# Fewer idle matmuls, and the load of v, its copies and two softmax steps moved, in an attention + feed-forward kernel on Trainium2

## Chip, cores, metric

The kernel runs on one core of one Trainium2 chip. The metric is the device time of one execution in microseconds (us).

In the profile's lines PE is the tensor engine (matmuls), PEld its weight loads, DVE VectorE, ACT ScalarE, POOL GpSimd and SP SyncE; L424 is line 424 of the kernel. `...` marks lines left out.

## The reference

Cross-covariance attention over the channels, then a feed-forward layer with a tanh GELU. There are 4 batches of 6080 rows and 256 channels; the hidden width is 2048.

```python
qn = q / (norm(q, axis=1) + 1e-6);  kn = k / (norm(k, axis=1) + 1e-6)
s = kn.transpose(0, 2, 1) @ qn / tau          # 256 x 256 for each batch
a = exp(s - s.max(-1));  a /= a.sum(-1) + 1e-9
x = (v @ a).reshape(24320, 256)
out = gelu_tanh(x @ w_in) @ w_out
```

The kernel folds `a @ w_in` into one matrix aW for each batch, so that a block of 512 rows of v needs one product with aW (first product) and one with W_out (second product, done with seven smaller products).

## The kernel before

Only the parts that the argument touches. At the start the Gram matrix of batch 0 is built from seven chunks of q and k, as they land. `warm(n)` issues n matmuls on zeros, whose results nobody reads, to keep the tensor engine busy.

```python
WARM = [0, 6, 10, 12, 14, 14, 0]
for c in range(nch):                    # nch = 7 chunks of batch 0
    ...                                 # loads, casts
    if 1 <= c < nch - 1:
        ss_rows(c - 1, 0); ss_rows(c - 1, 1)   # column sums of the squares, on the tensor engine
        warm(WARM[c])
    squares(0, c); fold_rows(0, c)
    if c == nch - 2:
        ss_rows(c, 0)
    if c == nch - 1:
        ss_rows(c, 0); q_factor(); ss_rows(c - 1, 1)
    for i in range(len(rows_of(0, c))):
        gram_row(0, c, i)
    if c == nch - 1:
        ss_rows(c, 1)
...                                     # loads of W_in, v, W_out: see the diff
pe_vt(0, "r")       # v of block 0: 8 transposes on the tensor engine, 2 copies on VectorE
warm(14)
scores(0)           # ACT: lnk, rk; VectorE: S = G * rk; ACT: eT = exp(S * rq)
first_aw()          # row sums of eT, aW of batch 0
```

Then 48 blocks of 512 rows (448 in the last of each batch) run, each in eight steps p. Step p of block n does a part of the first product of block n and of the second product of block n - 1. In between, the next batch is prepared: its chunks are loaded, squared and multiplied in blocks 0 to 8 of the batch, its norms taken in block 9 (`k_row` leaves the diagonal matrix dg), its exponentials in block 10 (`scores_c` does a reciprocal of a quarter in each of four steps, and eT in the last), and aW in block 11.

```python
if blk == 9:
    if p == 3: ss_cols(nxt); norms(nxt)
    if p == 7: k_row(nxt)
if blk == 10:
    if p == 0: k_row_pe(nxt)            # tensor engine: broadcast of dg (L350)
    if p == 1: scores_b(nxt)            # ACT: tanh
    if p in (2, 4, 6, 7): scores_c(nxt, (2, 4, 6, 7).index(p))
if blk == 11:
    if p == 0: row_sums(nxt)            # tensor engine: sums of eT (L386)
    aw_part(nxt, p // 2, p % 2, ...)
```

A record per line follows: L213 Gram rows, L231 and L237 sums of squares, L322 idle matmuls, L285 and L288/L289 transposes of v and their copies, L261 and L263 the logarithm and the factor rk of the k norms on ScalarE, L267 scores, L302 row sums of batch 0, L400 aW, L424 first product, L520 second product, L536 and L544 its additions and transpositions on VectorE.

Of the kernel before, what the change touches and what calls it, by code (L numbers as in the profile page):

```python
# [17 lines left out]
def kernel(  # L18
# [102 lines left out]
    def load_qk(b, c):  # L121
        load_one(b, c, 0)
        load_one(b, c, 1)
# [134 lines left out]
    def scores(b):  # L258

        lnk = smx.tile([128, 256], FP32, tag="lnk")  # L260
        nc.scalar.activation(lnk, SS[1], AF.Ln, bias=eps)  # L261
        rk = smx.tile([128, 256], FP32, tag="rk")
        nc.scalar.activation(rk, lnk, AF.Exp, scale=-0.5)  # L263
        S = smx.tile([128, 2, 256], FP32, tag="S")
        eT = smx.tile([128, 2, 256], BF16, tag="eT")
        for jc in range(2):
            nc.vector.tensor_mul(S[:, jc, :], G[b][:, jc, :], rk)  # L267
        for jc in range(2):
            nc.scalar.activation(eT[:, jc, :], S[:, jc, :], AF.Exp, scale=RQ[0][:, jc : jc + 1])
        ET[b] = eT  # L270
# [3 lines left out]
    def load_v0(n):  # L274
        t = yout.tile([128, BLK // 128, C], BF16, tag="ot", name=f"v{n}")
        V0.append(t)
        nc.gpsimd.dma_start(out=t, in_=v[0, n * BLK : n * BLK + BLK, :].rearrange(
            "(s p) c -> p s c", p=128))

    def pe_vt(n, tag):  # L280

        ps = pM.tile([128, 2, BLK], BF16, tag=tag, name=f"vt_ps{n}")
        for s in range(BLK // 128):
            for cc in range(2):
                nc.tensor.transpose(ps[:, cc, s * 128 : s * 128 + 128],  # L285
                                    V0[n][:, s, cc * 128 : cc * 128 + 128], ident_bf)
        vT = vts.tile([128, 2, BLK], BF16, tag="vT", name=f"vT_pe{n}")
        nc.vector.tensor_copy(vT[:, 0, :], ps[:, 0, :])  # L288
        nc.vector.tensor_copy(vT[:, 1, :], ps[:, 1, :])  # L289
        vt_tiles[n] = vT  # L290
# [27 lines left out]
    def warm(n):  # L318

        w = pH.tile([128, 2, 512], FP32, tag="h", name="warm")  # L320
        for i in range(n):
            nc.tensor.matmul(w[:, 0, 0:256], lhsT=ones_bf, rhs=zeros_bf, start=True, stop=True)  # L322
# [42 lines left out]
    def scores_c(b, step):  # L365

        th = TH[b]
        if step == 0:
            dn = smx.tile([128, 2, 256], FP32, tag="S")
            DN[b] = dn  # L370
            nc.vector.tensor_scalar(dn, th, -1.0, 1.0, op0=ALU.mult, op1=ALU.add)
        dn = DN[b]
        piece = dn[:, step // 2, step % 2 * 128 : step % 2 * 128 + 128]
        nc.vector.reciprocal(piece, piece)  # L374
        if step == 3:
            eT = smx.tile([128, 2, 256], BF16, tag="eT")
            nc.vector.scalar_tensor_tensor(eT, th, 1.0, dn, op0=ALU.add, op1=ALU.mult)
            ET[b] = eT
# [247 lines left out]
    with tc.manual_schedule():  # L626
        first = load_first()
        load_qk(0, 1)
        load_qk(0, 2)
        ident = const.tile([128, 128], FP32)  # L630
        make_identity(nc, ident)
        ones_bf = const.tile([128, 128], BF16)
        nc.vector.memset(ones_bf, 1.0)
        zeros_bf = const.tile([128, 256], BF16)
        nc.vector.memset(zeros_bf, 0.0)
        ones_f = const.tile([128, 128], FP32)
        nc.vector.memset(ones_f, 1.0)
        eps = const.tile([128, 1], FP32)
        nc.vector.memset(eps, 1e-12)
        halves = const.tile([128, 4], FP32)  # L640
        nc.vector.memset(halves, 0.5)
        log_it = const.tile([128, 1], FP32)
        nc.vector.memset(log_it, math.log(inv_tau))
        ident_bf = const.tile([128, 128], BF16)
        nc.vector.tensor_copy(ident_bf, ident)
        nc.scalar.preload_act_table_set("natural_log_exp_and_others")

        win_bf = const.tile([128, 2, D], BF16)
        wcomb = const.tile([128, 7, 8, 128], BF16)
        nch = len(chunks_of(0))  # L650
        WARM = [0, 6, 10, 12, 14, 14, 0]
        for c in range(nch):
            if c == 0:
                cast_first(first)
            if c >= 3:
                load_qk(0, c)
            if 1 <= c < nch - 1:
                ss_rows(c - 1, 0)
                ss_rows(c - 1, 1)
                warm(WARM[c])  # L660
            squares(0, c)
            fold_rows(0, c)
# [4 lines that stand above are left out]
                q_factor()  # L667
                ss_rows(c - 1, 1)
            for i in range(len(rows_of(0, c))):
                gram_row(0, c, i)  # L670
            if c == nch - 1:
                ss_rows(c, 1)
        wi = moe_w_in.rearrange("(c p) d -> p c d", p=128)
        for fs in range(4):
            nc.gpsimd.dma_start(out=win_bf[:, :, fs * 512 : fs * 512 + 512],
                                in_=wi[:, :, fs * 512 : fs * 512 + 512])
            if fs == 0:
                load_v0(0)
        load_v0(1)
        load_wout()  # L680
        load_v0(2)
        pe_vt(0, "r")
        warm(14)
        scores(0)
        first_aw()
        nc.scalar.preload_act_table(AF.Gelu_apprx_tanh)
        aw_part(0, 1, 0, "dve", "a")
        aw_part(0, 1, 1, "dve", "r")

        NN = B * NB  # L690
        for n in range(NN):
            b, blk = divmod(n, NB)
            nxt = b + 1
            for p in range(PAIRS):
                if n >= 1:
                    keeps(n - 1, p)
                if p == 0 and PE_BLOCKS <= n + 2 < NN:
                    load_vt(n + 2)
                gate = mm1(n, p)
                if n == 1 and p in (0, 3):  # L700
                    prep_wout(2 + p // 3)
                if p == 0 and n + 3 < NN:
                    cast_v(n + 3, gate)
                if n == 0 and p in (1, 3):
                    fs = 2 + p // 2
                    aw_part(0, fs, 0, "dve", "q")
                    aw_part(0, fs, 1, "dve", "p")
                if n == 0 and p in (6, 7):
                    prep_wout(p - 6)
                if n >= 1:  # L710
                    mm2(n - 1, p)
                    if p == 1:
                        sums_2(n - 1, 4, 8)
                        if n == 1:
                            prep_wout(4)
                    if p == PAIRS - 1:
                        store(n - 1)
                if p == 5:
                    sums_1(n)
                    if n + 1 < PE_BLOCKS:  # L720
                        pe_vt(n + 1, "q")
                if p == 7:
                    sums_2(n, 0, 4)
                if nxt < B:
                    ncn = len(chunks_of(nxt))
                    if p in (2, 5) and blk < ncn:
                        load_one(nxt, blk, p // 5, gate)
                    c = blk - 1
                    if 0 <= c < ncn:
                        if p == (4 if n == 1 else 0):  # L730
                            squares(nxt, c)
                        if p >= 2:
                            gram_row(nxt, c, p - 2)
                        if p == (6 if n == 1 else 3):
                            sum_rows(nxt, c)
                    if blk == 9:
                        if p == 3:
                            ss_cols(nxt)
                            norms(nxt)
                        if p == 7:  # L740
                            k_row(nxt)
                    if blk == 10:
                        if p == 0:
                            k_row_pe(nxt)
                        if p == 1:
                            scores_b(nxt)
                        if p in (2, 4, 6, 7):
                            scores_c(nxt, (2, 4, 6, 7).index(p))
                    if blk == 11:
                        if p == 0:  # L750
                            row_sums(nxt)
                        aw_part(nxt, p // 2, p % 2, "act" if p in (1, 4, 5, 6) else "dve")
        mm2_last(NN - 1)
# [35 lines left out]
```

## Time and profile before

| | before |
|---|---|
| median of 4 runs | 726.29 us (726.0 to 726.41) |
| span of the profiled run | 724.6 us |
| tensor engine busy | 693.5 us, 96% |
| granted clock | 1.000 |

The prediction below shows the main lines: the engines, the chain that ended last, the tensor engine's waits and the start's timeline. Three more places come from the timeline of the kernel before; the columns are start us, us, engine, line, operation, tiles, shapes, count, and in brackets the idle time ahead and what ended it.

```profile
41.40 1.89 PE L424 MATMUL hp<-vT_pe,aw 128*128 128x512 bf16 x8
...
61.95 1.03 PE L520 MATMUL r<-t,wcomb 128*128 128x256 bf16 x8 [0.70 <-DVE c L536]
...
183.92 0.70 PE L350 MATMUL ps<-dg,ones_f 128*128 128x256 f32 x2 [0.60 <-DVE dg L344]
```

The first block's products begin at 41.40. At 61.95 the tensor engine still waits for VectorE, which has been busy without a gap since 48.9. After that, all its waits of note are the two kinds at each batch change, of which 183.92 is one.

### The profile page before, as it was taken

The page shows a single profiled execution, that of the slowest core. Times are in us where ns is not written, and L with a number is a line of the kernel's source. Part 1 is how long each engine was busy: PE and PEld are TensorE (multiplying, and loading weights), DVE is VectorE, ACT ScalarE, POOL GpSimd, SP SyncE. Part 2 cuts the span into 40 slices and gives each one's busy share as a digit, 9 for nine tenths or more (in the row PEclk, how much of TensorE's full clock was granted, in tenths as well). Part 3 has the DMA queues.
Part 4 walks back from the last instruction along what each step waited for, and adds up shares of the span by engine and source line. Part 5 has one row for each costly group of instructions (what it writes and reads, how often), then busy time and mean ns, then how long its engine had stood idle before and what let it go on. Part 6 is the DMA issues. An engine that isn't in the chain of part 4 may idle for free.

```text
span 724.6 us, 12205 instructions
## 1 busy us (share of the span) xinstructions
PE 693.5 (96%) x4808; PEld 472.0 (65%) x4896; DVE 508.8 (70%) x904; ACT 486.0 (67%) x593; POOL 70.2 (10%) x131
## 2 busy tenths in 40 slices
PE   3899999999899999999999999999999999999997
PEld 2756666666566666666666666666665666666665
DVE  4479878785866787878676878778587465564565
ACT  4377667766667677667667776677666767666673
POOL 4221011100001111010000111011000000000000
PEclk9999999999999999999999999999999999999999
DMA  9995968963548788786436887889344546546233
GB/s 241 201 245 91 157 108 137 140 100 57 91 71 135 115 140 133 122 120 100 72 59 93 137 140 116 131 125 126 57 71 75 86 58 97 79 78 96 43 59 56
DMA packets 161706, 78.93 MB, mean 109 GB/s; under 512 B 149408, under 2 KB 152736, under 8 KB 160672
## 3 DMA queue, kind: packets, MB, share of 16 engines
q0 software_dynamic: 13936, 39.46, 34.6%
q1 hardware_dynamic: 147088, 37.52, 31.4%
q10 hardware_dynamic: 624, 1.16, 0.5%
q8 instruction: 38, 0.62, 0.3%
q14 instruction: 20, 0.16, 0.1%
HBM read 78.91 MB, written 36.57 MB: 159 GB/s over the span
## 4 chain that ended last, share of the span: by engine, by line
PE 87%; DVE 6%; DMA 4%; issue 1%; POOL 1%; ACT 0%; DVEq 0%; POOLq 0%
PE hp L424 41%; PE r L520 22%; PE p L520 11%; PE q L520 6%; PE G L213 4%; DMA t<-in_k_dram 2%; DMA v<-in_v_dram 2%; PE ps L400 2%; DVE ot L544 1%; DVE dn L374 1%; DVE t L504 1%; DVE t L502 1%; DVE t L503 1%; DVE c L536 0%; POOL t L93 0%
## 5 line engine op out<-in xcount | busy, mean ns | idle before, releaser
L428 ACT ACTIVATE g<-hp 128x1024 bf16<-128x1024 f32 (+1 forms) x384 | 387.4, 1015 | 200.6 <-PE hp L424 186.8
L424 PE MATMUL hp<-vT,aw 128*128 128x512 bf16 (+1 forms) x1363 | 353.9, 377 | 2.7
L520 PEld LDWEIGHTS <-wcomb 128*128 128x128 bf16 x2688 | 262.6, 98 | 98.8 <-issue 1.8
L424 PEld LDWEIGHTS <-aw 128*128 128x128 bf16 x1536 | 150.0, 98 | 109.3 <-issue 1.1
L520 PE MATMUL r<-t,wcomb 128*128 128x256 bf16 (+1 forms) x1152 | 148.1, 271 | 1.2 <-DVE c L536 0.7
L536 DVE TENSOR_TENSOR c<-r,y 128x256 f32<-128x256 f32 (+1 forms) x95 | 40.1, 422 | 58.3 <-PE r L520 51.0
L536 DVE TENSOR_TENSOR c<-q,x 128x256 f32<-128x256 f32 (+1 forms) x48 | 20.0, 417 | 71.6 <-PE q L520 69.8
L213 PE MATMUL G<-t 128*128 128x256 bf16 (+1 forms) x368 | 64.8, 273 | 1.1 <-DMA t<-in_k_dram 1.1
L504 DVE TENSOR_TENSOR t<-t,g 128x1024 bf16<-128x1024 bf16 (+1 forms) x96 | 65.2, 679 | 0.0
L503 DVE TENSOR_TENSOR t<-g 128x1024 bf16<-128x1024 bf16 (+1 forms) x96 | 65.0, 677 | 0.0
L502 DVE TENSOR_TENSOR t<-g,t 128x1024 bf16<-128x1024 bf16 (+1 forms) x96 | 63.5, 661 | 0.0
L544 DVE STREAM_TRANSPOSE ot<-c 128x256 f32<-128x256 f32 (+1 forms) x144 | 57.6, 425 | 1.7
L491 DVE TENSOR_TENSOR t<-g 128x2048 bf16<-128x2048 bf16 (+1 forms) x48 | 57.8, 1204 | 0.0
L132 POOL DMA_DIRECT2D vb<-in_v_dram x45 | 22.6, 502 | 359.0 <-PE hp L424 359.0
L520 PE MATMUL r<-g,wcomb 128*128 128x256 bf16 (+1 forms) x384 | 49.3, 271 | 1.4
L165 ACT ACTIVATE sq<-t 128x1536 bf16<-128x1536 bf16 (+3 forms) x29 | 43.7, 1506 | 9.8 <-DMA t<-in_q_dram 9.8
L520 PE MATMUL p<-g,wcomb 128*128 128x256 bf16 (+1 forms) x384 | 49.3, 271 | 0.0
L520 PE MATMUL q<-g,wcomb 128*128 128x256 bf16 (+1 forms) x384 | 49.3, 271 | 0.0
L520 PE MATMUL p<-t,wcomb 128*128 128x256 bf16 (+1 forms) x384 | 49.3, 271 | 0.0
L544 DVE STREAM_TRANSPOSE ot<-r 128x256 f32<-128x256 f32 (+1 forms) x48 | 21.3, 443 | 33.1 <-PE r L520 33.1
L213 PEld LDWEIGHTS <-t 128*128 128x128 bf16 (+1 forms) x368 | 35.5, 98 | 11.2 <-issue 2.7
L529 ACT ACTIVATE y<-p 128x256 f32<-128x256 f32 (+1 forms) x95 | 36.3, 382 | 0.7 <-ACT x L529 0.4
(101 smaller groups left out, 341.2 us busy)
## 6 DMA issues: line engine op xcount, KB each, us to landing
out_dram<-ot SPq DMA_DIRECT2D x176, 128.0 KB, 2.8
vb<-in_v_dram POOLq DMA_DIRECT2D x41, 256.0 KB, 5.2
t<-in_q_dram POOLq DMA_DIRECT2D x22, 384.0 KB, 4.9
t<-in_k_dram POOLq DMA_DIRECT2D x22, 384.0 KB, 4.5
wst<-in_moe_w_out_dram POOLq DMA_DIRECT2D x2, 1024.0 KB, 9.8
t<-in_q_dram POOLq DMA_DIRECT2D x3, 512.0 KB, 15.0
t<-in_k_dram POOLq DMA_DIRECT2D x3, 512.0 KB, 16.9
out_dram<-ot SPq DMA_DIRECT2D x12, 112.0 KB, 3.6
```

Source lines behind the costliest of these rows:

```text
L165: nc.scalar.activation(sq[:, 0:n, 0:256], qt[:, 0:n, :], AF.Square)
L213: nc.tensor.matmul(G[b][:, jc, :], lhsT=qt[:np_, r, jc * 128 : jc * 128 + 128], rhs=kt[:np_, r, :], start=first and jc == 0, stop=last and ...
L424: mm = nc.tensor.matmul(hp[:, u, :cols], lhsT=AW[b][:, cc, fc * 128 : fc * 128 + 128], rhs=vt_tiles[n][:, cc, :cols], start=cc == 0, stop= ...
L428: nc.scalar.activation(GS[n][:, 2 * p : 2 * p + 2, :cols], hp[:, :, :cols], AF.Gelu_apprx_tanh)
L491: nc.vector.tensor_sub(t1[:, :, :hc], quarter(n, 0, 1), quarter(n, 0, 0))
L502: nc.vector.tensor_sub(v[2], b22, v[1])
L503: nc.vector.tensor_sub(v[3], b22, quarter(n, 0, 1, f0, f1))
L504: nc.vector.tensor_sub(v[4], v[2], quarter(n, 1, 0, f0, f1))
L520: nc.tensor.matmul(ACCS[n, acc][:, :hc], lhsT=wcomb[:, w, fc, :], rhs=x, start=first and fc == 0, stop=fc == 7, skip_group_check=True)
L529: nc.scalar.activation(x[:, :hc], ACCS[n, acc][:, :hc], AF.Copy)
L536: nc.vector.tensor_add(CS[n][:, tj, ci, :hc], ACCS[n, acc][:, :hc], XS[n, name][:, :hc])
L544: nc.vector.transpose(OT[n][:, tj * nb : tj * nb + nb, ci, :], src.rearrange("p (x t) -> p x t", t=32))
```

## The change

The intent has three parts: fewer idle matmuls at the start (28 fewer in all); v of block 0 loaded ahead of W_in and its transposes and copies put behind the scores; and the norms and exponentials of later batches one or two steps sooner, so that the tensor engine finds them ready.

```diff
-        WARM = [0, 6, 10, 12, 14, 14, 0]
+        WARM = [0, 4, 8, 8, 10, 4, 0]
...
+        load_v0(0)
         for fs in range(4):
             nc.gpsimd.dma_start(out=win_bf[:, :, fs * 512 : fs * 512 + 512],
                                 in_=wi[:, :, fs * 512 : fs * 512 + 512])
-            if fs == 0:
-                load_v0(0)
         load_v0(1)
         load_wout()
         load_v0(2)
+        warm(8)
+        scores(0)
         pe_vt(0, "r")
-        warm(14)
-        scores(0)
         first_aw()
...
-                        if p == 7:
+                        if p == 6:
                             k_row(nxt)
...
-                        if p in (2, 4, 6, 7):
-                            scores_c(nxt, (2, 4, 6, 7).index(p))
+                        if p in (2, 3, 4, 6):
+                            scores_c(nxt, (2, 3, 4, 6).index(p))
```

## The prediction

> **What bounds the kernel now.** I read the page first, then the waits of the tensor engine, then the timeline at the start and around one batch change. The page says that the tensor engine is busy for almost the whole span, at full granted clock, and the chain that ended last is mostly its two product lines:
>
> ```profile
> PE 693.5 (96%) x4808; PEld 472.0 (65%) x4896; DVE 508.8 (70%) x904; ACT 486.0 (67%) x593; POOL 70.2 (10%) x131
> PE 87%; DVE 6%; DMA 4%; issue 1%; POOL 1%; ACT 0%; DVEq 0%; POOLq 0%
> ```
>
> So after the start-up, time comes off only where the tensor engine stands still. Its waits (total us, times, longest us) say where that is:
>
> ```profile
> PE G L213 <- DVE first L118: 10.4, 1, 10.4
> PE ps L386 <- DVE eT L377: 4.4, 3, 1.5
> PE ps L350 <- DVE dg L344: 1.8, 3, 0.6
> PE ss L231 <- DVE a L177: 1.5, 3, 0.7
> PE G L213 <- DMA t<-in_k_dram: 1.1, 1, 1.1
> PE r L520 <- DVE c L536: 0.7, 1, 0.7
> PE vt_ps L285 <- DMA v<-in_v_dram: 0.5, 1, 0.5
> ```
>
> The second and third are three equal waits each, one per batch change (the batch that starts next gets its norms, L350, and its exponentials' row sums, L386). The change aims at both. The rest lies in the first 62 us. The timeline of the start (start us, us, engine, line, instruction) shows what the wait list hides, since idle matmuls count as busy:
>
> ```profile
> 31.99 1.69 PE L322 MATMUL warm<-zeros_bf,ones_bf 128*128 128x256 bf16 x14
> 33.52 0.44 PE L231 MATMUL ss<-ones_bf,sq 128*128 128x1 bf16 x12
> 33.82 1.47 PE L213 MATMUL G<-t 128*128 128x256 bf16 x12
> 36.74 0.47 ACT L261 ACTIVATE lnk<-ss,eps 128x256 f32<-128x256 f32 x1 [0.74 <-PE ss L237]
> 37.25 0.42 ACT L263 ACTIVATE rk<-lnk 128x256 f32<-128x256 f32 x1
> 37.88 0.42 DVE L288 COPY vT_pe<-vt_ps 128x512 bf16<-128x512 bf16 x1 [3.67 <-PE vt_ps L285]
> 38.22 0.41 DVE L289 COPY vT_pe<-vt_ps 128x512 bf16<-128x512 bf16 x1
> 38.55 0.75 DVE L267 TENSOR_TENSOR S<-G,rk 128x256 f32<-128x256 f32 x2
> ```
>
> From 31.34 to 36.70 the tensor engine has no gap: 14 idle matmuls stand in front of real work. And the scores S wait for the two v copies, though their factor rk is there at 37.67.
>
> **What the Trainium skill says.** (1) "TensorE: Matmul & The Clock Gate", Part 1: the array runs at half clock after an idle window of about 3.4 us and at full clock after a busy one. That is what the idle matmuls are for. The trace agrees on the cold start: the first sixteen Gram matmuls take 3.59 us, later sixteens 1.91. It shows no return to half clock later. (2) Same page, "Back-to-back issue gap": N/2.4 + 2.5 ns, 109 ns at N = 256. The trace has (33.52 - 31.99)/14 = 109 ns. (3) Same page, "Architectural detail": VectorE is strict FIFO, so where an instruction stands in its queue decides; the S that waits behind the v copies agrees. (4) "DMA: Bandwidth & Descriptors", "Two DMAs through the same engine are not ordered": within one queue of one DMA engine descriptors start in order. The landings agree (issue time plus time to landing): k of the last chunk 33.8, W_in part 0 35.8, v of block 0 37.2, W_in parts 1 to 3 38.5, 39.9, 41.0, v of block 1 42.3, W_out 45.4 and 48.4; each was issued 9 to 15 us earlier, so they are spaced by bandwidth, not by issue.
>
> **The change, part by part.**
>
> *A. Idle matmuls.* 28 go: 2, 2, 4, 4, 10 in the loop and 6 before the first aW. Those before chunks 1 to 4 stand ahead of waits for k or for squares, so I give them nothing. The ten before the sum rows of chunk 5 are followed by work whose data are there: the q squares end at 32.06, k of chunk 5 lands by 32.4, its squares end at 33.34, q and k squares of chunk 6 at 33.67 and 34.20. Removing 10 x 0.109 = **1.09 us** puts these stages at 32.42, 32.72, 34.03, 34.13, 34.79 and 35.23, each after its data. So lnk starts at 35.65 instead of 36.74.
>
> *B. v copies behind the scores.* rk is then ready at 36.57. S no longer waits for the copies: it starts at 36.60, not 38.55. That is 1.95 earlier, of which 1.09 is A and **0.86** is B. The copies (0.42 + 0.33) run from 37.35 to 38.1. The reciprocal of the sums, which stood 1.73 after S, comes at 38.33, so they fit. The idle matmuls (now 8, 0.87 us, to 36.5) and the transposes of v (about 0.5) fit ahead of the exponentials (eT ready at 37.6).
>
> *C. v ahead of W_in.* v and W_in part 0 are 256 KB each on landing and swap places, so v should land by 35.8 and W_in part 0 at about 37.2, when v landed before. Part 0 is needed at 37.65 (39.60 less 1.95), part 1 at 38.6 and lands at 38.5. The margins are 0.4 and 0.1. I take off **0.1** for the second.
>
> Start: the first block's matmuls begin at 39.5 instead of 41.40, **1.85** earlier. Then VectorE is the bound from 48.9 to 61.9 (v copies, W_out preparation, sums). That chain ends the tensor engine's 0.7 us wait at 61.95. It needs the second half of W_out at 50.22, less 1.9 is 48.3, and that lands at 48.4. Another **0.1** goes: **1.75 us** from the start.
>
> *D. k_row at p = 6 instead of 7* (block 9 of a batch). It held 0.95 us of VectorE from 182.91 to 183.86, behind the three t sums. It now stands before the last transposition and those sums, at 180.13, ready at 181.1. The norms' root ended at 176.8. The tensor engine wants dg at 182.29 + 8 x 0.109 = 183.16 and got it at 183.92: **0.76 us** per batch (the page's 0.60 counts from the matmul's modelled end).
>
> *E. The exponentials at p = 2, 3, 4, 6 instead of 2, 4, 6, 7* (block 10). The four reciprocals of 0.91 to 0.95 us are the same:
>
> ```profile
> 189.69 0.91 DVE L374 RECIPROCAL dn<-dn 128x128 f32<-128x128 f32 x1
> 194.37 0.91 DVE L374 RECIPROCAL dn<-dn 128x128 f32<-128x128 f32 x1
> 197.28 0.94 DVE L374 RECIPROCAL dn<-dn 128x128 f32<-128x128 f32 x1
> 198.25 0.69 DVE L377 SCALAR_TENSOR_TENSOR eT<-th,dn 128x512 bf16<-128x512 f32 x1
> 199.00 0.25 PE L386 MATMUL ps<-ones_bf,eT 128*128 128x1 bf16 x4 [1.47 <-DVE eT L377]
> ```
>
> The second stays at 189.69; the third fills the gap of 1.08 us before the addition at 191.68; the fourth is then at 194.37 and eT ends at 195.97 instead of 198.94. The row sums could go at 196.50 + 8 x 0.109 = 197.37 and went at 199.00: **1.63 us** per batch. VectorE's three t sums slip by 0.75 to 198.0, before the row sums' reciprocal is due. One new constraint: the last transposition now follows eT and frees r, which the first product of the next block wants at 196.50. It ends at about 196.36. It fits by about 0.1.
>
> D and E: 3 x (0.76 + 1.63) = 7.17; I keep **7.1**. With the start 1.75: 8.85. 726.26 - 8.85 = **717.4 us**, 1.2% less.
>
> **The rivals.**
> 1. *The clock falls.* With fewer idle matmuls the wait before chunk 4 grows from 1.07 to about 1.6 us, with another gap of 0.7 behind that chunk. For: it is the one thing they protect. Against: no gap comes near 3.4 us. If it happened, some 3.4 us at half clock would cost 1 to 2 us: about 719.
> 2. *A transfer takes the wait's place.* W_in parts 0 and 1 or the second W_out half land as the bytes of one queue allow, whatever the tensor engine does. Margins are 0.4, 0.1 and none. If v does not land sooner, or W_in slips by 0.5 to 1 us, half of the start's gain goes: about 718.3. k of the next batch is another: needed at 56.10, less 1.9, landing at about 54.5; but the 0.7 us wait at 61.95 absorbs it.
> 3. *VectorE becomes the bound at a batch change.* k_row and eT now stand ahead of transpositions that free r. If r comes late, or the additions at 191.68 and 193.34 slip, each batch loses 0.1 to 0.5: up to 1.5 us, about 718.5. For: a margin of 0.1. Against: VectorE had idle time of 1.08 us just there.
> 4. *Only the start gains* (D and E given back later), about 724.5. The tensor engine waits for almost nothing after 62 us except in D and E, so this is unlikely.
>
> **Range and chances.** The estimate is 717.4. All of it right without the small deductions gives 717.1; half the start lost plus 0.3 per batch gives 719.2. I choose 716.4 to 719.4. 2% is 14.5 us, more than all waits that the change touches (4.4 + 1.8 + 0.7 + 0.5 and 28 idle matmuls at 0.109 us, 10.5 in all), so within 2% has 0.98.
>
> **What would show it.** A: lnk near 35.65. B: S near 36.6, with the v copies after it. C: v lands by 36, no wait for W_in over 0.2 us, first block matmul near 39.5. Clock: chunk 4's sixteen matmuls still 1.9 us. D and E: no L350 or L386 lines among the tensor engine's waits, and no new wait for r over 0.1 us. The prediction is wrong if W_in or the clock takes the start back, or if r takes the batch changes back.

## The result, and the profile after

| | before | after |
|---|---|---|
| median of 4 runs | 726.29 us | 716.64 us (716.49 to 716.79) |
| ratio | | 0.9868 (95%: 0.9851 to 0.9885) |
| span of the profiled run | 724.6 us | 714.7 us |
| tensor engine busy | 693.5 us, 96% | 693.7 us, 97% |
| granted clock | 1.000 | 0.999 |
| first block's products begin | 41.40 us | 39.12 us |

A ratio is the mean time of one kernel's fast runs over that of the other's in the same rounds, so it is not quite the ratio of the medians quoted. All outputs are right.

The tensor engine's waits in the changed kernel (what waited, for what, total us, times, longest us):

```profile
PE G L213 <- ACT first L116: 10.3, 1, 10.3
PE ss L231 <- DVE a L177: 2.1, 3, 0.7
PE G L213 <- DMA t<-in_k_dram: 1.2, 1, 1.2
PE r L520 <- DVE c L536: 0.7, 1, 0.7
PE sums L302 <- ACT eT L269: 0.7, 1, 0.7
PE hp L424 <- ACT g L428: 0.2, 1, 0.2
```

The lines for L386 and L350 are gone, and nothing has come in their place: every wait left is in the first 60 us. The wait for v (L285) is gone too. The start of the changed kernel, from its timeline:

```profile
31.65 0.60 PE L322 MATMUL warm<-zeros_bf,ones_bf 128*128 128x256 bf16 x4
32.09 0.44 PE L231 MATMUL ss<-ones_bf,sq 128*128 128x1 bf16 x12
...
35.31 0.47 ACT L261 ACTIVATE lnk<-ss,eps 128x256 f32<-128x256 f32 x1 [0.74 <-PE ss L237]
...
36.26 0.75 DVE L267 TENSOR_TENSOR S<-G,rk 128x256 f32<-128x256 f32 x2 [2.47 <-ACT rk L263]
36.94 0.41 DVE L288 COPY vT_pe<-vt_ps 128x512 bf16<-128x512 bf16 x1
...
39.12 1.89 PE L424 MATMUL hp<-vT_pe,aw 128*128 128x512 bf16 x8
...
59.68 1.03 PE L520 MATMUL r<-t,wcomb 128*128 128x256 bf16 x8 [0.70 <-DVE c L536]
```

S now waits for rk and nothing else, and the copies of v stand behind it. The wait for VectorE's addition stays, 2.27 us sooner. The first batch change:

```profile
180.00 1.04 PE L520 MATMUL r<-g,wcomb 128*128 128x256 bf16 x8
180.88 0.60 PE L350 MATMUL ps<-dg,ones_f 128*128 128x256 f32 x2
181.31 1.03 PE L424 MATMUL hp<-vT,aw 128*128 128x512 bf16 x4
...
193.35 1.04 PE L520 MATMUL r<-g,wcomb 128*128 128x256 bf16 x8
194.22 0.24 PE L386 MATMUL ps<-ones_bf,eT 128*128 128x1 bf16 x4
```

L350 and L386 follow the products ahead of them at once (180.00 + 0.88, 193.35 + 0.87).

### The profile page after: what moved, and what is told of

The parts are those of the page before. It is cut to its first block, busy times and chain, and to the rows that moved or that the text cites. A ratio compares the mean times of both kernels' runs of the same rounds, so it can differ in the third digit from the quotient of the medians.

```text
span 714.7 us, 12238 instructions
## 1 busy us (share of the span) xinstructions
PE 693.7 (97%) x4868; PEld 469.7 (66%) x4868; DVE 508.2 (71%) x904; ACT 485.9 (68%) x593; POOL 70.1 (10%) x131
## 3 DMA queue, kind: packets, MB, share of 16 engines
q10 hardware_dynamic: 624, 1.16, 0.5%
## 4 chain that ended last, share of the span: by engine, by line
PE 92%; DMA 4%; DVE 3%; issue 0%; ACT 0%; POOL 0%; DVEq 0%; POOLq 0%
PE hp L424 45%; PE r L520 23%; PE p L520 11%; PE q L520 6%; PE G L213 5%; DMA t<-in_k_dram 2%; PE ps L400 2%; DMA t<-in_q_dram 1%; DVE ot L544 0%; PE ss L244 0%; DVE sq L166 0%; DVE c L536 0%; PE ss L237 0%; PE ps L350 0%; DVE t L504 0%
## 5 line engine op out<-in xcount | busy, mean ns | idle before, releaser
L424 PE MATMUL hp<-vT,aw 128*128 128x512 bf16 (+1 forms) x1440 | 363.0, 377 | 0.0
```

The source lines that it names most:

```text
L424: mm = nc.tensor.matmul(hp[:, u, :cols], lhsT=AW[b][:, cc, fc * 128 : fc * 128 + 128], rhs=vt_tiles[n][:, cc, :cols], start=cc == 0, stop= ...
```

## The experiments

Theory: the change's five parts act where the prediction puts them, and add up, except that the start's parts (fewer idle matmuls, copies behind the scores, v ahead) need each other. Rivals: the batch change profits from the start, or one of its two moves is enough; a transfer takes back the start's gain; the clock falls.

### Only the batch change

Edit: the kernel before with the last two hunks of the diff alone.

> The kernel before with only the two moves at the batch change (k_row at p = 6, the exponentials at p = 2, 3, 4, 6). Theory, the parts add: the waits for dg and for eT disappear and the three batch changes give 7.5 us (2.50 each, as the two traces differ there), so about 718.8 us, with the start unchanged (first matmul of block 0 at 41.4 us, row products of block 1 after the 0.7 us wait near 62 us). Rival, the earlier start opens room that these moves need: then clearly less than 7.5 us, 720 us or more.

Measured: 718.73 us against 726.19 (ratio 0.9898, 0.9881 to 0.9914), 7.5 us less. L350 and L386 do not appear among the waits, and the first block begins at 41.38. The theory holds: this part needs nothing from the start.

### Only the start

Edit: the changed kernel with `k_row` at p = 7 and the exponentials at p in (2, 4, 6, 7) again.

> The changed kernel with the batch change put back as before. Theory, the parts add: only the start's 2.28 us, so about 724.0 us, with the waits for dg 1.8 us and for eT 4.4 us back. Rival, part of the start's gain is given back at the first batch change, because that stage waits for data and not for the tensor engine: then 725 us or more.

Measured: 724.17 us against 726.19 (ratio 0.9975, 0.9960 to 0.9990), 2.0 us less. With the run above, 7.5 + 2.0 = 9.5 us of the 9.65 us of the whole. The parts add, and the start's gain crosses the batch changes without loss: the first block begins 2.11 us sooner (39.29), and the row sums of the later batches 2.12, 2.13 and 2.14 us sooner than before.

### Only k_row sooner

Edit: the kernel before with the `if p == 7` hunk alone.

> The kernel before with only k_row moved to p = 6. Theory: the wait for dg goes, 0.76 to 0.87 us per batch, the wait for eT stays at 1.47 us each: 723.7 to 724.0 us. Rival, the exponentials hang on dg, so an earlier dg makes eT earlier too: then the wait for eT falls as well, by 0.8 us a batch, and the time is about 721.5 us.

Measured: 723.56 us (one run; before 726.19). The tensor engine's waits:

```profile
PE G L213 <- ACT first L116: 10.3, 1, 10.3
PE ps L386 <- DVE eT L377: 4.4, 3, 1.5
PE r L520 <- DVE c L536: 0.7, 1, 0.7
...
```

The wait for dg is gone and the wait for eT stands unchanged at 4.4 us. eT does come sooner with dg, but the tensor engine moves up by as much: from one row sum product to that of the next batch it takes 171.95 us instead of 172.82, 0.87 less. So this rival falls.

### Only the exponentials sooner

Edit: the kernel before with the `scores_c` hunk alone.

> The kernel before with only the exponentials moved to p = 2, 3, 4, 6. Theory: the wait for eT goes, 1.63 us per batch, the wait for dg stays at 0.60 us each: about 721.4 us. Rival: without the earlier dg the third reciprocal meets the addition at p = 5, and a wait for c takes the place of some of it: 722.5 us or more, with a new wait of r for c in the tensor engine's list.

Measured: 721.64 us (one run), 4.6 us less. The wait for dg stays at 1.8 us in three, the wait for eT is gone, and there is no new wait for c (0.7 us once, near 62 us, as before). From row sums to row sums it is 171.23 us instead of 172.82, 1.59 less. The two moves together gave 7.5 us; their single runs give 2.6 + 4.6 = 7.2.

### Only the idle matmuls

Edit: the kernel before with the `WARM` line of the change and `warm(8)` for `warm(14)`.

> The kernel before with only the 28 idle matmuls taken out; v is still loaded after the first part of W_in and copied ahead of the scores. Theory: the logarithm of the k norms starts about 1.1 us sooner (ten idle matmuls of 109 ns ahead of the sum rows of chunk 5), but v lands at about 37.2 us as before and the scores stand behind its copies, so nearly nothing of it reaches the end: 726.0 us, within 0.3 of before. Rival: the idle matmuls are worth their own time whatever else is there: 725.1 us. Third: the clock falls and the time rises to 727 us or more.

Measured: 725.92 us against 725.92 (ratio 0.9997, 0.9980 to 1.0013). Nothing. Its start:

```profile
35.56 0.47 ACT L261 ACTIVATE lnk<-ss,eps 128x256 f32<-128x256 f32 x1 [0.74 <-PE ss L237]
...
37.17 0.62 PE L285 MATMUL vt_ps<-ident_bf,v 128*128 128x128 bf16 x8 [1.65 <-DMA v<-in_v_dram]
...
38.50 0.75 DVE L267 TENSOR_TENSOR S<-G,rk 128x256 f32<-128x256 f32 x2
```

The logarithm starts 1.2 us sooner than before (36.74), but the time saved has become a wait for v: 1.65 us instead of 0.51. The scores stand behind v's copies and start where they did (38.50, before 38.55). The 28 matmuls of 109 ns, 3.1 us of busy tensor engine, were worth nothing by themselves.

### Only the copies behind the scores, twice

Edit: the kernel before with `warm(14); scores(0); pe_vt(0, "r")` in this order, v still loaded after the first part of W_in.

> The kernel before with only the order of v's transposes and the scores changed (the 14 idle matmuls ahead of both, v still loaded after the first part of W_in). Theory: the scores start when rk is there, 37.7 instead of 38.55, 0.86 us sooner; the tensor engine runs its 14 idle matmuls to 38.3 us and the transposes to 38.8 us and is ready for the sums at 38.7 to 38.8 us: 725.4 us. Rival: v's copies then end after the reciprocal of the sums is due and take the place of the scores' wait: no gain, 726.2 us.

Measured, in one run: 725.64 us, against 725.92. The first block began at 40.37, 1.0 us sooner, but a new wait stood where the next batch's first Gram row wants its k:

```profile
56.28 0.38 PE L213 MATMUL G<-t 128*128 128x256 bf16 x2 [1.05 <-DMA t<-in_k_dram]
```

That looked like a bound which takes the start's gain back. So it was run again, with a kernel beside it that loads v of block 2 after this k instead of ahead of it.

> The kernel of the copies alone once more, timed. In its one run the first block began 1.0 us sooner than before, yet the time fell by only about 0.3 us, and the first Gram row of the next batch waited 1.05 us for k. Theory: that wait is a bound that follows from the earlier start (k lands when the bytes of its queue allow): it comes again, between 0.5 and 1.1 us, and the time is 725.4 to 725.8 us. Rival: that landing was a chance of one run: no wait over 0.3 us and 725.2 us.

Measured: 725.52 us against 726.24 (ratio 0.9992, 0.9977 to 1.0007), with no wait for k at all in the profiled run, and a first block at 40.63. The rival held as to the wait: that landing was one of its run. As to the time it did not, since 725.52 lies in the range that the theory gave. In the first profile k landed 8.5 us after its issue, in the second 6.5. The interval includes no change; the 0.7 us between the medians agrees with the 0.77 us by which the first block began sooner.

### v of block 2 loaded later

Edit: on the kernel above.

```diff
-        load_v0(2)
...
                         load_one(nxt, blk, p // 5, gate)
+                        if n == 0 and p == 5:
+                            load_v0(2)
```

> The same kernel with the load of v of block 2 issued after the k load of the next batch instead of ahead of it, which takes 256 KB out of k's way. Theory, k's landing takes back part of the start's gain: k lands about 1.1 us sooner, the wait for k falls below 0.2 us, the 0.7 us wait for VectorE's addition returns, and the time falls to about 725.2 us, 0.3 to 0.5 under the kernel without this. Rival: the wait is not one for bytes ahead in the queue: k lands as late as before and nothing changes.

Measured: 725.62 us against 726.24 (ratio 0.9994, 0.9979 to 1.0008), so no gain over its neighbour's 725.52. k did land sooner, 5.3 us after its issue instead of 6.5. But k was not waited for, and the wait for VectorE's addition grew from 0.7 to 1.0 us. A miss, and the timeline shows where it comes from (the same view under "Three things more").

### v not ahead of W_in

Edit: the changed kernel with the load hunk undone.

> The changed kernel with v of block 0 loaded after the first part of W_in again, all else as changed. Theory: v lands 1.0 to 1.4 us after the first part of W_in, near 37 us, where the transposes want it at 36.0 us: they wait about 1 us, the sums behind them start about 0.3 to 0.6 us later than 37.3 us: 717.0 us. Rival: nothing waits for v long enough, since the sums wait for the exponentials until 37.3 us anyway: 716.6 us. Third: the swap is also what makes the whole stream of W_in land about 1 us sooner, and then 717.5 us or more.

Measured: 716.83 us against 725.92 (ratio 0.9875, 0.9860 to 0.9889), where the changed kernel had 0.9868. The difference is smaller than the intervals, so the time alone settles nothing. The trace does, for the start:

```profile
36.97 0.62 PE L285 MATMUL vt_ps<-ident_bf,v 128*128 128x128 bf16 x8 [0.71 <-DMA v<-in_v_dram]
37.43 0.19 PE L302 MATMUL sums<-ones_bf,eT 128*128 128x1 bf16 x2
```

The transposes wait 0.71 us for v, but the sums start only 0.15 us later than with the swap (37.28), since they wait for the exponentials anyway. Part of the third theory shows too: without the swap v and the first part of W_in are both there about 3.5 us after the last k, at 36.9; with it, about 2.6 us after, at 36.0. The tensor engine does not wait for either in the changed kernel. Without the swap its weight loads also wait 0.26 us at 38.32 for the second part of W_in (landed at 38.3, with the swap at 37.3), and the first block begins at 39.38 instead of 39.12 (0.12 us of this is a later start of chunk 4's squares, 28.48 instead of 28.36).

This run also shows how the start's parts need each other. The first block begins at 41.40 before, at 41.35 with the idle matmuls alone, at 40.37 and 40.63 with the copies alone, at 39.38 with both, and at 39.12 with the load of v moved too. Chunk 4's start moves such times by up to 0.5 us from run to run. The load of v alone was not run.

### No idle matmuls

Edit: the changed kernel with `WARM` all zero and no `warm(8)`.

> The changed kernel with no idle matmuls at all. Theory, the clock matters: stretches of 2 to 3 us with little work let the clock fall in the start-up, matmuls of 128x256 then stand 213 ns apart instead of 109, and the first block starts 0.5 to 2 us later than 39.1 us: 717 to 718.5 us. Rival, the idle matmuls are not needed: the sums of chunk 5 start up to 0.4 us sooner still and the time is about 716.2 us.

Measured: 716.98 us (716.69 to 718.51) against 725.92 (ratio 0.9880, 0.9865 to 0.9894). The clock did fall, in the tensor engine's timeline:

```profile
15.57 3.54 PE L213 MATMUL G<-t 128*128 128x256 bf16 x16
...
19.69 1.91 PE L213 MATMUL G<-t 128*128 128x256 bf16 x16
...
28.36 2.97 PE L213 MATMUL G<-t 128*128 128x256 bf16 x16 [2.25 <-DMA t<-in_k_dram]
```

The sixteen Gram matmuls of chunk 4 take 2.97 us where the changed kernel takes 1.91, and four sums behind them 1.01 instead of 0.60. The trace's record of the granted clock agrees: full to 29.0 us, half to 32.4, full again after. It fell 0.7 us after the work had begun again, not in the gap. Even so the first block begins at 39.29, 0.17 us later than with idle matmuls. The sums behind chunk 4 start only 0.13 us later (31.13 instead of 31.00), since the changed kernel waits 0.72 us for VectorE just there; and their own 0.41 us more is about what the 4 matmuls ahead of chunk 5 had cost. The first line is no evidence: chunk 1 ran at half clock, wholly or in part, in nine of the fourteen traces (2.86 to 3.55 us; 2.01 in the others), also with all idle matmuls in place. So the idle matmuls do what they are for, and at this length of start it is worth little. One of the four runs was at 718.51, which was not seen with the others. Its mean granted clock, 0.995, is that of the run of 716.69 too, so the clock does not account for it; the cause stays open.

### The squares later

What is left after the start is the 0.70 us wait at 59.68. In the order of VectorE's queue, 0.92 us of squares of the next batch stand just ahead of the addition that ends it. Edit, on the changed kernel:

```diff
-                        if p == (4 if n == 1 else 0):
+                        if p == (6 if n == 1 else 0):
                             squares(nxt, c)
...
-                        if p == (6 if n == 1 else 3):
+                        if p == (7 if n == 1 else 3):
                             sum_rows(nxt, c)
```

> The changed kernel with the first squares of the next batch in block 1 at p = 6 instead of 4 and their sums at p = 7 instead of 6. Theory, the 0.70 us wait near 59.7 us is VectorE's queue order alone (0.92 us of squares stand ahead of the addition that the tensor engine waits for, 2.2 us of sums ahead of a transposition): the wait goes, with two gaps of about 0.25 behind it, and the time falls by 0.7 to 1.2 us, to 715.4 to 715.9 us. Rival: the wait moves to the next addition or to a transposition, 716.4 us or more.

Measured: 716.0 us against 726.24 (ratio 0.9861, 0.9845 to 0.9878). That is 0.6 us under the changed kernel's median, which ran in other rounds, and by their intervals the two can't be told apart. In the traces the second block's third product (q) begins at 68.1 instead of 69.1, and in the third block at 82.9 instead of 83.5. So 1.0 us is gained and about 0.4 given back one block on, where the postponed sums meet the next addition:

```profile
74.41 0.81 PE L520 MATMUL r<-t,wcomb 128*128 128x256 bf16 x6 [0.28 <-DVE c L536]
```

Both the theory (the wait is queue order) and the rival (it moves on) are half right.

### Three things more

Edit: the kernel above, with `WARM = [0, 4, 8, 8, 10, 0, 0]` and v of block 2 loaded after k, as in the earlier experiment.

> The changed kernel with three things more: those squares and sums later, no idle matmuls before the sum rows of chunk 5 (4 fewer), v of block 2 loaded after k of the next batch. Theory: 0.7 to 1.2 us from the squares and up to 0.35 us from the idle matmuls (the q squares end 0.35 us after the point where they would be wanted), k in time because less stands in its way: 715.0 to 715.5 us, the fastest of all. Rival: the start's gain meets the landing of k or of W_out and only the squares' gain is left: 715.4 to 715.9 us. If the clock falls: over 716 us.

Measured: 715.91 us (715.69 to 715.92) against 726.24 (ratio 0.9859, 0.9844 to 0.9874): the lowest median of all, but level with the kernel above. The theory (715.0 to 715.5) missed; the rival's time came, but not from the landing that it named. The first block begins at 38.95, 0.29 us sooner than there; 0.04 of it is left at 68 us. VectorE's timeline of this kernel, with the issue of the postponed load beside it:

```profile
46.85 0.77 POOL L277 DMA_DIRECT2D v<-in_v_dram  x1
47.18 0.95 DVE L468 CAST wcomb<-wst 128x1024 bf16<-128x1024 f32 x1
48.05 1.21 DVE L469 TENSOR_TENSOR wf_a<-wst,wst 128x1024 f32<-128x1024 f32 x1
```

And the same cast in the changed kernel, where that load was issued long before:

```profile
47.35 0.68 DVE L468 CAST wcomb<-wst 128x1024 bf16<-128x1024 f32 x1
```

The cast takes 0.95 us instead of 0.68 while GpSimd issues the load, and in this stretch VectorE is the bound, so 0.27 us goes to the end of it. The load moved in the earlier experiment did the same (0.95 us); in the other twelve traces the cast takes 0.68 or 0.69. The Trainium skill has a reason, "Advanced Engine Details and Errata", "VectorE Performance Modes": VectorE's second port to SBUF is shared with GpSimd, and two-port VectorE instructions and GpSimd's instructions block each other. The two traces agree with it. That the moved load slows the cast is shown, since the earlier experiment and its neighbour differ in that load alone; that the port is the reason, and that this cast uses both ports, no run shows.

## Why the prediction was right, point by point

The measured 716.64 us lies in the range of 716.4 to 719.4, 0.8 us under the 717.4 named. Of that, 0.4 is in the batch changes and 0.5 in the start, by the traces (together 0.1 more than the medians show).

- *A, idle matmuls:* the logarithm was to start at 35.65 and started at 35.31. The 1.09 us came out exactly; the remaining 0.34 us is k of chunk 4, whose squares start at 28.36 instead of 28.70. Over the fourteen traces this start lies at 28.34 to 28.61 (mean 28.47) in the seven with fewer idle matmuls and at 28.37 to 28.84 (mean 28.64) in the seven with all. So about half of the 0.34 us is spread between runs, which is luck, and whether the other half belongs to the change stays open. What the step didn't say outright is that A alone is worth nothing, as its own experiment shows; it was counted only together with B and C.
- *B, copies:* 0.86 us predicted. S starts 2.29 us sooner than before, which is 0.34 + 1.09 + 0.86.
- *C, the transfers:* the step that was mis-sized. v and W_in were to swap places at 35.8 and 37.2 us. Issue plus time to landing gives 34.7 and 36.0, and 37.3 instead of 38.5 for the second part of W_in. So the deduction of 0.1 us for that part was not needed (without the swap it would have been: there that part was waited for), nor the one for W_out, whose second half was taken up without a wait at 47.95. Landing times from one trace were read as fixed by bandwidth; with the same bytes in another order they moved by about a microsecond.
- *VectorE as the bound to 62 us:* held. The 0.70 us wait is still there after the change, so the start's 2.28 us at the first block is 2.27 us at that wait. The runs that change VectorE's queue confirm the bound: a cast slower by 0.27 us made the wait 0.26 us longer (0.96 with v of block 2 later), and with the squares moved it went.
- *D and E:* from one row sum product to that of the next batch, 172.82 us (199.00 to 371.82) became 170.31 (194.22 to 364.53): 2.51 us for each batch, 7.5 in all, where 2.39 and, rounded down, 7.1 were predicted. The sum missed one term: the broadcast of dg and the product after it stand 0.54 us apart when the first waits (183.92 to 184.46), and 0.43 when it doesn't (180.88 to 181.31). That is 0.11 us per batch, and k_row alone gave the 0.87 = 0.76 + 0.11 (the exponentials alone 1.59, for 1.63). The margin of 0.1 for r held: the transposition that frees it ends at 193.22, the product starts at 193.35.
- *Rivals:* the clock did not fall in the changed kernel (chunk 4 takes 1.91 us), and where it was made to fall, for 3.4 us, the first block began 0.17 us later, net of the idle matmuls left out: far less than the 1 to 2 us estimated. The transfers took nothing. A new VectorE wait at the batch change did not come.

## What to carry to other kernels

Where one engine is busy 96% of the time, read its list of waits and work out for each from which queue position the missing result comes; a move of one or two steps in another engine's queue was worth 0.9 and 1.6 us here each time it occurs. Idle work in front of real work doesn't show as a wait, and taking it out pays only if what comes behind it does not wait for something else: alone it gave 0, with the copies and the load moved the start gave 2.0 us. A landing time in one trace is a sample, so before a wait for a transfer is called a bound, profile again.

## What the Trainium skill lacked or had wrong

- "TensorE: Matmul & The Clock Gate" gives an idle window of about 3.4 us for the fall to half clock. In the kernel without idle matmuls the clock fell although the longest gap before chunk 4 was 2.25 us, with 0.8 us of small matmuls and a gap of 0.72 us ahead of it: sixteen matmuls took 2.97 us instead of 1.91. In the 3.4 us up to the fall (25.6 to 29.0) the tensor engine was busy for 1.16 us. The page does name frequent short idle times as a second cause, but not how much work within a window keeps the clock up.
- "DMA: Bandwidth & Descriptors" says in what order descriptors of one queue start, but nothing was found there on how the order of two loads of equal size changes the time of both. Here v and the first part of W_in were both there about 2.6 us after the last k in the five traces with v first, and 2.9 to 3.6 us after it in the nine with W_in first. The reason stays open.
